# Seven-product multiplication at a second level inside the first matrix stage of an attention and feed-forward kernel

## The chip, the cores and the metric

The kernel runs on one core of a Trainium2 chip, as one program. The metric is the device time of one execution in microseconds (us), lower is better. TensorE (PE) does the matrix products, VectorE (DVE) and ScalarE (ACT) do elementwise work and read the accumulators, GpSimd (POOL) and SyncE (SP) start transfers.

## The reference

```python
kv  = einsum('bhsd,bhse->bhde', k, v)            # q, k, v: (8, 8, 576, 64)
o   = einsum('bhsd,bhde->bhse', q, kv)
x   = o / sqrt(mean(o*o, -1) + 1e-6) * g_norm    # then (B,H,S,D) -> (4608, 512)
h   = x @ w_in                                   # w_in: (512, 2048)
g   = s * max(h, 0)**2 + b
out = g @ w_out                                  # w_out: (2048, 512)
```

All is float32. Most of the arithmetic is in the two products with `w_in` (first stage) and `w_out` (second stage).

## The kernel before, in words

The 4608 tokens are cut into nine **units** of 512 tokens (`u` = 0 to 8). Each unit does the first stage, then the second. Beside it runs the attention of the next unit, as two halves A and B; each is a chain: `turn` (DVE transposes q), `product` (64 short matmuls), `back` (two DVE transposes out of PSUM), `square` (ACT), `row_sum` (DVE, then a root on ACT), `norm` (DVE), `turn_x` (DVE), `scale` (ACT).

Both stages use Strassen's scheme in Winograd's form: a 2 x 2 block product with seven products in place of eight, and sums around them. Blocks of the left matrix are combined into S1 to S4, those of the right into T1 to T4. Unit 0 multiplies plainly in the first stage. From unit 1 on the first stage has one level of the scheme: A is `w_in` transposed (A11, A12, A21, A22), B is the unit's x (B11 to B22, 256 tokens wide). The products are numbered 1 = A11 B11, 2 = A12 B21, 3 = S4 B22, 4 = A22 T4, 5 = S1 T1, 6 = S2 T2, 7 = S3 T3. The second stage of units 2 to 8 has two levels (`at_two_levels`, L878).

The first stage goes in four **steps** `s` (256 rows of each half of the result per step), each with seven **large products**. A large product (`mm1_product`) is four matmuls with a moving operand of 256 columns; the profile shows each float32 matmul as two records, so it is 8 records of 128x256. Products 1, 6, 5, 3 of a step add up in one PSUM bank x (two such banks in turn), 7 and 4 in one bank y (two in turn), 2 has its own bank z (one). Between the products on x, ACT copies the bank out (L706) and the next product on it waits for that copy. DVE makes the four blocks of the result from them (`add`, L250) and applies the squared relu (`relu_sq`, L658). The last step's products 3 and 4 are laid into the second stage (`rest`, L1137), between its first small products. There the order is: product 1 of top-level group 1 (`do_1(1)`), the large products 3 and 4, then `do_1(2)`, `do_1(6)`, `go_1(7)`, `do_1(5)`. `sums_1` makes the four sums for that group on DVE; in the kernel before it is called between the last step's products 7 and 5.

The order of the work is written out by hand: every engine takes its instructions in the order in which the program text issues them, and semaphores make it wait for another engine's instruction. `sides` (L1405) is the table that says before which product of which step each part of the attention chain is issued. The weights of the second stage come through a ring of 14 places in SBUF (`pump`, `used`), filled by transfers on SP's queue in a fixed order, a place being reused when all before it are done. Eight of the places hold k and v for `kv_product` in the units that have it (1 to 6).

Of the kernel before, what the change touches and what calls it, by code (L numbers as in the profile page):

```python
# [16 lines left out]
def kernel(  # L17
# [231 lines left out]
    def add(o, a, b):  # L249
        nc.vector.tensor_tensor(out=o, in0=a, in1=b, op=ALU.add)  # L250
# [42 lines left out]

    w2_dram = [dram.tile([P, 2, FC // 2, P], FP32, name=f"w2_{i}") for i in range(8)]
    w3_dram = [dram.tile([P, 4, FC // 4, P], FP32, name=f"w3_{i}") for i in range(8)]
    w_up = convp.tile([P, FC // 2, DM], FP32, name="w_up")
    w_dn = convp.tile([P, FC // 2, DM], FP32, name="w_dn")
    W2_AT = {
# [474 lines left out]

    ring = {}
    NR = 14

# [14 lines left out]
    for u in range(1, U):  # L793
        if u in kv_due:
            queue_w2 += [(u, "kv", (n, m)) for n in range(NP) for m in range(2)]
        if u == 1:
            queue_w2 += [(u, i, n) for i in (1, 2, 6, 7, 5, 3, 4) for n in range(2)]
        else:
            queue_w2 += [(u, i, m) for i, m in ORDER]
    next_at = [0]  # L800

# [3 lines left out]
    def pump():  # L805

        while queue_w2 and sum(map(size_of, held)) + size_of(queue_w2[0]) <= NR:
            u, i, n = key = queue_w2.pop(0)
            held.append(key)
            t = late["ring"][:, next_at[0] : next_at[0] + size_of(key)]  # L810
            next_at[0] = (next_at[0] + size_of(key)) % NR
            if i == "kv":
                load_kv_into(t[:, 0], kv_due[u], *n)
                continue
            t = t[:, :, : 2 * HN].rearrange("p q (f n) -> p q f n", n=P)
            if u == 1:
                nc.sync.dma_start(out=t, in_=w2_dram[i][:, :, 4 * n : 4 * n + 4])
                ring[key] = t
                continue
            if n <= 3:  # L820
                f = 4 if n > 1 else 0
                src = w2_dram[i][:, n // 3, f : f + 4]
            else:
                src = w3_dram[i][:, n - 4]
            nc.sync.dma_start(out=t[:, 0], in_=src)
            ring[key] = t[:, 0]
# [525 lines left out]
    def side_of(A, B, sums, u):  # L1352

        if u == 0:
            return {
                6: [lambda: kv_product(1)],
                7: [partial(A["turn"], 0), partial(A["turn"], 1)],
                8: [A["product"], A["back"], A["square"]],
                9: [A["row_sum"], partial(B["turn"], 0), partial(B["turn"], 1)],
                10: [A["norm"], A["turn_x"], A["scale"], B["product"], B["back"], B["square"]],  # L1360
                11: [B["row_sum"], B["norm"]],
                12: [B["turn_x"], B["scale"], lambda: [fn() for fn in sums_w_in(0)]],
                13: [sums],
            }
        return {
            0: [A["scale"]],
            1: [B["turn"]],
            4: [B["product"], B["back"], B["square"]],
            5: [B["row_sum"]],
            6: [B["norm"]],  # L1370
            8: [B["turn_x"], B["scale"]],
            11: [sums],
            13: [partial(loads, 3, 1)],
        }

    def loads(u, i):

        if u < U:
            for load in load_q(4 * u + 2 * i):
                load()  # L1380
# [24 lines left out]
    def sides(u, A, B):  # L1405

        first, second = {}, {}
        kv = []  # L1410
        if u in kv_due:
            kv.append(lambda: kv_product(kv_due[u]))
            kv.append(lambda: used(*((u, "kv", (n, m)) for n in range(NP) for m in range(2))))
        q = {half: [partial(loads, u + 2, half)] for half in range(2)}
        if u == 1:
            for s in range(1, NS):
                first[((0, 1), (0, 3), (1, 1))[s - 1]] = list(sums_w_in(s))
            first.update({
                (1, 3): kv,
                (2, 0): [partial(A["turn"], 0), partial(A["turn"], 1)],  # L1420
                (2, 1): [A["product"]],
                (2, 2): [A["back"]],
                (2, 3): [A["square"]],
                (3, 0): [A["row_sum"]],
                (3, 2): [A["norm"], A["turn_x"]],
                (3, 3): [lambda: [load() for load in load_q(12, rest_on=nc.sync)]],
            })
            return first, second
        if u + 1 == U:
            return first, second  # L1430
        if u == 2:
            first = {
                (0, 2): [A["turn"]],
                (0, 3): kv,
                (1, 1): [A["product"]],
                (1, 2): [A["back"], B["turn"]],
                (1, 3): [A["square"]],
                (2, 0): [A["row_sum"]],
                (2, 1): [B["product"]],
                (2, 2): [A["norm"], A["turn_x"]],  # L1440
                (2, 3): q[0],
                (3, 0): [B["back"], A["scale"]],
                (3, 1): [B["square"]],
            }
            second = {
                0: [B["row_sum"]], 2: [B["norm"]], 3: [B["turn_x"], *q[1]],
                "sums": [B["scale"]],
            }
        else:
            first = {  # L1450
                (0, 0): [A["turn"]],
                (0, 1): [A["product"]],
                (0, 2): [A["back"]],
                (0, 3): [A["square"], B["turn"]],
                (1, 0): [A["row_sum"]],
                (1, 1): kv,
                (1, 2): [A["norm"], A["turn_x"]],
                (1, 3): [B["product"], *q[0]],
                (2, 0): [B["back"], A["scale"]],
                (2, 1): [B["square"]],  # L1460
                (2, 2): [B["row_sum"]],
                (2, 3): [B["norm"]],
                (3, 0): [B["turn_x"], *q[1]],
                (3, 1): [B["scale"]],
            }
        second[5], second[6] = [[lambda n=n: x_sums(u + 1)[n]()] for n in range(2)]
        return first, second

    for u in range(U):
        A, B = pairs_of(u + 1) if u + 1 < U else (None, None)  # L1470
        if u == 0:
            first_unit()
            second = mm2(0)
        else:
            if u == 1:
                loads(2, 0)
                loads(2, 1)
            steps = [mm1(u, s) for s in range(NS)]
            first, at_second = sides(u, A, B)
            second = mm2(u, steps[-1], at_second) if u > 1 else mm2(u)  # L1480
        for s in range(NS if u > 0 else 0):
            a = steps[s]

            def at(n):
                for fn in first.get((s, n), []):
                    fn()

            at(0)
            a["x1"]()
            if s:  # L1490
                x3(steps[s - 1])
            a["z2"]()
            at(1)
            if s:
                y4(steps[s - 1])
            a["x6"]()
            at(2)
            a["y7"]()
            if s == NS - 1 and u > 1:
                second["sums"]()  # L1500
            at(3)
            a["x5"]()
        if u > 1:
            second["rest"]()
            continue
        side = side_of(A, B, lambda: [fn() for fn in x_sums(u + 1)], u)
        for n, slot in enumerate(second):
            slot()
            if u == 0:
                if n == 1:  # L1510
                    for i in range(2):
                        load_kv(1, i, convp, tag="raw", bufs=3)
                    store_w2(1)
                    loads(1, 0)
                    loads(1, 1)
                    store_w2(5)
                elif n == 2:
                    t2 = convp.tile([P, 4 * R * D], FP32, name="w_t2", tag="raw", bufs=3)
                    W2_AT[6] = t2[:, : FC // 2 * HN].rearrange("p (f n) -> p f n", n=HN)
                    for i in range(14, 16):  # L1520
                        more(i)
                    sub_w_out(6, 3, 5)
                    store_w2(3, 2, 6)
            if n == 0 and u > 0:
                x3(steps[-1])
                y4(steps[-1])
            for step in side.get(n, []):
                step()
        if u == 0:
            tc_late()  # L1530
            pump()
# [30 lines left out]
```

## Time and profile before

| what | value |
|---|---|
| median of 3 timed runs | 920.17 us (920.1 to 920.28) |
| the profiled execution | 919.9 us, its span 918.1 us |
| granted TensorE clock | 1.00 |
| PE busy | 907.6 us (99%) in 7272 matmul records |
| DVE busy | 678.2 us (74%) |
| ACT busy | 210.3 us (23%) |
| first product of units 6 and 7 | starts at 629.48 and 726.96 us: one unit is 97.48 us |
| first stage of unit 6, to the end of the last step's product 5 (629.60 to 679.50 us) | PE busy throughout; DVE 35.78, ACT 15.27 us |
| the rest of unit 6 (679.50 to 727.00 us) | PE busy throughout; DVE 37.91, ACT 4.34 us |

A row of the timeline gives start, length, engine, line, operation, tile written<-tiles read, shapes, the count of instructions merged into it and, in brackets, the idle time before it and what ended that. The length of a matmul row includes its run through the array, so the pace of PE is read from one start to the next. In the groups, the second number behind the bar is the mean time of one instruction in ns.

### The profile page before, as it was taken

The numbers are of one execution on the slowest core, as the hardware profiler recorded it, in microseconds if no ns is written. First come the engines' busy times: TensorE is split into PE (matmuls) and PEld (weight loads), VectorE is DVE, ScalarE is ACT, GpSimd is POOL, SyncE is SP. The second block draws the span as 40 slices with busy tenths as digits, with TensorE's granted clock in tenths as the row PEclk, the third lists the DMA queues.
The fourth block names the chain that finished last, engine by engine and source line by source line (L and its number), as shares of the span: only waits on it lengthen the run. The fifth ranks groups of instructions, "written<-read, shape, count | busy, mean of one in ns | idle before, by whom it ended". The sixth has DMA issues, their size and how long they took to land.

```text
span 918.1 us, 18306 instructions
## 1 busy us (share of the span) xinstructions
PE 907.6 (99%) x7272; PEld 824.6 (90%) x7272; DVE 678.2 (74%) x1149; ACT 210.3 (23%) x386; POOL 220.2 (24%) x412
## 2 busy tenths in 40 slices
PE   7999999999999999999999999999999999999998
PEld 7888888888889998899889988998899988998898
DVE  2789777687577985887677867787678768864685
ACT  3774132211124013310232023301330034002200
POOL 2000017012703242711273025603440300020000
PEclk9999999999999999999999999999999999999999
DMA  9777937249922993189416953496428800890086
GB/s 258 228 280 259 270 94 238 85 102 349 322 66 64 277 319 110 30 251 310 153 39 184 297 164 108 119 292 229 116 58 286 282 6 12 272 308 18 12 253 184
DMA packets 113605, 167.70 MB, mean 183 GB/s; under 512 B 28400, under 2 KB 45552, under 8 KB 113520
## 3 DMA queue, kind: packets, MB, share of 16 engines
q1 hardware_dynamic: 95504, 141.98, 49.4%
q0 software_dynamic: 14560, 22.31, 8.4%
q10 hardware_dynamic: 3456, 2.23, 0.9%
q8 instruction: 58, 0.95, 0.4%
q14 instruction: 27, 0.22, 0.1%
HBM read 142.35 MB, written 24.12 MB: 181 GB/s over the span
## 4 chain that ended last, share of the span: by engine, by line
PE 96%; DVE 2%; DMA 1%; ACT 0%; issue 0%; SPq 0%; DVEq 0%
PE x_ps L91 51%; PE y_ps L91 29%; PE z_ps L91 11%; PE kv_ps L380 2%; PE y_ps L559 2%; DMA kv_sb<-in_v_dram 1%; PE qT_ps L548 0%; DVE xn L469 0%; SPq L107 0%; DVE ss L459 0%; DVE o L861 0%; DVE sub L253 0%; DVE wb L245 0%; DVE xn L592 0%; DVE a L253 0%
## 5 line engine op out<-in xcount | busy, mean ns | idle before, releaser
L1380 POOL DMA_DIRECT2D q_sb<-in_q_dram x256 | 143.6, 569 | 149.6 <-issue 118.9
L706 ACT COPY r<-x_ps 128x512 f32<-128x512 f32 x96 | 56.0, 584 | 453.2 <-PE x_ps L91 423.4
L970 POOL DMA_DIRECT2D out_dram<-o x110 | 54.8, 505 | 400.7 <-DVE o L861 276.2
L91 PE MATMUL x_ps<-w_sb,sub 128*128 128x128 f32 x1176 | 149.3, 276 | 0.7 <-DVE r L861 0.7
L91 PEld LDWEIGHTS x_ps<-w_sb,sub 128*128 128x128 f32 x1176 | 139.7, 192 | 1.5 <-DVE r L861 0.9
L91 PE MATMUL x_ps<-xs,ws 128*128 128x256 f32 x512 | 122.3, 382 | 0.0
L91 PE MATMUL y_ps<-xs,wb 128*128 128x256 f32 x512 | 121.7, 380 | 0.0
L91 PEld LDWEIGHTS x_ps<-xs,ws 128*128 128x128 f32 x512 | 96.2, 190 | 16.5 <-issue 3.7
L91 PEld LDWEIGHTS y_ps<-xs,wb 128*128 128x128 f32 x512 | 96.7, 190 | 13.8 <-DVE s L250 0.4
L250 DVE TENSOR_TENSOR a<-y_ps,r 128x512 f32<-128x512 f32 x64 | 44.1, 689 | 83.2 <-ACT r L706 73.4
L91 PE MATMUL x_ps<-xT,wa 128*128 128x256 f32 x384 | 89.6, 380 | 0.1
L91 PEld LDWEIGHTS x_ps<-xT,wa 128*128 128x128 f32 x384 | 72.3, 190 | 10.1 <-ACT xT L503 0.5
L91 PE MATMUL x_ps<-w_sb,a 128*128 128x128 f32 (+1 forms) x432 | 64.9, 298 | 0.0
L91 PE MATMUL y_ps<-w_sb,a 128*128 128x128 f32 (+1 forms) x416 | 62.1, 295 | 0.0
L91 PEld LDWEIGHTS x_ps<-w_sb,a 128*128 128x128 f32 x432 | 59.0, 191 | 3.2 <-issue 0.4
L91 PE MATMUL x_ps<-xT,ws 128*128 128x256 f32 x256 | 61.2, 382 | 0.0
L91 PE MATMUL z_ps<-xT,wa 128*128 128x256 f32 x256 | 60.5, 379 | 0.0
L658 DVE SCALAR_TENSOR_TENSOR a<-a 128x512 f32<-128x512 f32 x82 | 56.7, 692 | 2.8
L91 PEld LDWEIGHTS y_ps<-w_sb,a 128*128 128x128 f32 x416 | 56.1, 192 | 2.1
L91 PEld LDWEIGHTS z_ps<-xT,wa 128*128 128x128 f32 x256 | 48.6, 190 | 6.6
L91 PEld LDWEIGHTS x_ps<-xT,ws 128*128 128x128 f32 x256 | 48.1, 190 | 6.5
L861 DVE SCALAR_TENSOR_TENSOR r<-x_ps,s_col,o 128x256 f32<-128x256 f32 (+1 forms) x84 | 34.7, 413 | 25.7 <-PE x_ps L91 24.5
(158 smaller groups left out, 1263.8 us busy)
## 6 DMA issues: line engine op xcount, KB each, us to landing
w_sb<-w SPq DMA_DIRECT2D x343, 256.0 KB, 4.8
w_raw<-in_moe_w_in_dram SPq DMA_DIRECT2D x8, 1024.0 KB, 7.3
w_raw<-in_moe_w_out_dram SPq DMA_DIRECT2D x8, 1024.0 KB, 5.2
w_sb<-w SPq DMA_DIRECT2D x14, 512.0 KB, 8.6
w<-sub POOLq DMA_DIRECT2D x28, 256.0 KB, 6.4
w_sb<-in_k_dram SPq DMA_DIRECT2D x24, 288.0 KB, 5.9
w_sb<-in_v_dram SPq DMA_DIRECT2D x24, 288.0 KB, 5.8
out_dram<-o POOLq DMA_DIRECT2D x92, 64.0 KB, 3.8
```

Of the source, the lines that this page charges most:

```text
L91: nc.tensor.matmul(o, lhsT=lhsT, rhs=rhs, start=start, stop=stop, skip_group_check=True)
L250: nc.vector.tensor_tensor(out=o, in0=a, in1=b, op=ALU.add)
L380: nc.tensor.matmul(ps[r][(r ^ l) * HB : (r ^ l) * HB + HB, i, :], lhsT=kv[l][0][rows, j, :], rhs=kv[l][1][rows, j, :], start=(j == 0), sto ...
L559: nc.tensor.matmul(ps[l][32 * p : 32 * p + 32, r, lo:hi], lhsT=bd_kv[b % 2][rows, p, at : at + 32], rhs=st["qT"][rows, p, lo:hi], start=Tr ...
L658: nc.vector.scalar_tensor_tensor(t, t, 0.0, t, ALU.max, ALU.mult)
L706: nc.scalar.copy(st[name], src)
L861: nc.vector.scalar_tensor_tensor(o, ps, s_col, other, ALU.mult, ALU.add)
L970: queues[s % 2].dma_start(out=view[b, jj, :, cols], in_=st[name, j][s * w : s * w + w, cols])
L1380: load()
```

## The change

From unit 2 on the first stage is done by a new function `mm1_deep`. Three of its large products per unit, each taken over a pair of steps, are multiplied at two levels: product 2 for the pair of steps 0 and 1 (key `(2, 0)`), product 3 for that pair (`(3, 0)`), and product 2 for steps 2 and 3 (`(2, 1)`). Each is seven **small products** of two matmuls with 128 columns (4 records). Their left sums are made once, beside unit 1's second stage, and written to DRAM (`sums_of_w_in`); six ring places per unit bring them back. Their right sums are made per unit (`sums_of_x`). All small products 1, 6, 5, 3 add up in one bank `sx`, 2, 4 and 7 in the one bank z; DVE reads these out and adds them onto what is already in the result's tile. What x1 and x5 leave in bank x is copied by ACT straight into the result's tiles. Where a block is complete only after the small products, the squared relu is two ACT instructions per step (`done_of`). The order of a pair of steps is written out in `run`, with numbered slots for the attention parts, and `sides` has new tables; `sums()` (start of `sums_1`) stands behind the last `x5`. Unit 8 has no attention work.

```diff
+    DEEP = ((2, 0), (3, 0), (2, 1))
+    def sums_of_w_in(key):
...
+        add(s1, a21, a22)
+        sub(s2, s1, a11)
+        sub(s3, a11, a21)
+        sub(s4, a12, s2)
+        for n in range(2):
+            nc.gpsimd.dma_start(
+                out=w1_dram[key][:, n], in_=t[n].rearrange("p f n -> p (f n)")
+            )
+    def mm1_deep(u):
...
+        def sums_of_x():
...
+            sub(t1, b12, b11)
+            sub(t2, b22, t1)
+            sub(t3, b22, b12)
+            sub(t4, b21, t2)
+        def x1(s):
+            st["x", s] = bank_of("x", "x")
+            mm1_product(1, u, s, st["x", s], True)
+            nc.scalar.copy(g_tile("a11", s), st["x", s])
...
+        def x5(s):
+            mm1_product(5, u, s, st["x", s], False)
+            nc.scalar.copy(g_tile("a21", s), st["x", s])
+            t = g_tile("a22", s)
+            add(t, st["y", s], ga["a21", s])
+            if s == NS - 1:
+                relu_sq_on_act(t)
+            else:
+                relu_sq(t)
...
+        def y4(s):
+            mm1_product(4, u, s, st["y", s], False)
+            t = g_tile("a12", s)
+            add(t, st["y", s], st["r2", s])
...
+        def small(i, pair, *ms):
...
+            for m in ms:
...
+                ps = st["sx" if m in (1, 6, 5, 3) else "sy"]
+                w, x = w_of(m), a[m][:, i - 2]
+                for b in range(2):
+                    matmul(ps[:, b], w[:, b], x, first and b == 0, True)
...
+                if m == 1:
+                    keep("q1", 0, 0)
+                elif m == 2:
+                    add(to(0, 0), ps, st["q1"])
+                elif m == 6:
+                    keep("q2", 1, 0)
+                elif m == 5:
+                    keep("q4", 1, 1)
+                    add(to(1, 1), st["sy"], st["q4"])
+                elif m == 3:
+                    add(to(0, 1), ps, to(0, 1))
+                elif m == 4:
+                    add(to(1, 0), ps, st["q2"])
+        def done_of(i, pair):
+            for s in (2 * pair, 2 * pair + 1):
+                relu_sq_on_act(ga[{2: "a11", 3: "a21"}[i], s])
+        def run(at, sums):
...
+            at(4)
+            y7(0)
+            small(2, 0, 6, 7)
+            at(5)
+            x5(0)
+            small(2, 0, 5)
+            at(6)
+            x6(1)
+            small(2, 0, 3, 4)
+            done_of(2, 0)
+            at(7)
+            y4(0)
+            at(8)
+            y7(1)
+            at(9)
+            x5(1)
+            at(10)
+            x1(2)
...
+            small(3, 0, 3, 4)
+            x6(3)
+            done_of(3, 0)
+            at(15)
+            small(2, 1, 1, 2)
+            x5(2)
+            at(16)
+            small(2, 1, 6, 7)
+            y7(3)
+            s1(0)
+            s1(1)
+            at(17)
+            small(2, 1, 5)
+            x3(2)
+            s3(0)
+            s3(1)
+            at(18)
+            small(2, 1, 3, 4)
+            done_of(2, 1)
+            y4(2)
+            s1(2)
+            s3(2)
+            x5(3)
+            sums()
...
+            queue_w2 += [(u, key, m) for key in DEEP for m in (6, 5)]
...
+            **{n: [partial(sums_of_w_in, key)] for n, key in zip((3, 7, 9), DEEP)},
...
             first = {
-                (0, 0): [A["turn"]],
-                (0, 1): [A["product"]],
-                (0, 2): [A["back"]],
-                (0, 3): [A["square"], B["turn"]],
-                (1, 0): [A["row_sum"]],
-                (1, 1): kv,
-                (1, 2): [A["norm"], A["turn_x"]],
-                (1, 3): [B["product"], *q[0]],
...
+                2: [A["turn"]],
+                4: [A["product"]],
+                5: [A["back"]],
+                6: [A["square"]],
+                7: [A["row_sum"], *kv],
+                8: [A["norm"], A["turn_x"]],
+                9: [B["turn"]],
+                10: [B["product"], *q[0]],
+                11: [B["back"], A["scale"]],
+                13: [B["square"]],
+                14: [B["row_sum"]],
+                15: [B["norm"]],
+                16: [B["turn_x"], *q[1]],
+                18: [B["scale"]],
             }
```

The last table is that of units 3 to 7. Unit 2 has its own, in which `turn` of B stands in slot 9 and its product in slot 12, `back` of B in slot 16.

More of the change, by code (lines that the diff above doesn't have):

```diff
@@ L295 @@
     w3_dram = [dram.tile([P, 4, FC // 4, P], FP32, name=f"w3_{i}") for i in range(8)]
+    DEEP = ((2, 0), (3, 0), (2, 1))
+    w1_dram = {key: dram.tile([P, 2, 4 * P], FP32, name=f"w1_{key[0]}{key[1]}") for key in DEEP}
     w_up = convp.tile([P, FC // 2, DM], FP32, name="w_up")
@@ L771, in mm1 @@
         )
+    def sums_of_w_in(key):
+        i, pair = key
+        w = [
+            (ws[s][:, 2] if i == 3 else wa[s][:, KH:])
+            for s in (2 * pair, 2 * pair + 1)
+        ]
+        a11, a12, a21, a22 = w[0][:, 0], w[0][:, 1], w[1][:, 0], w[1][:, 1]
+        t = [
+            late["sub"].tile([P, FC // 4, P], FP32, name="sub", tag="sub") for _ in range(2)
+        ]
+        (s2, s3), (s1, s4) = ((x[:, :2], x[:, 2:]) for x in t)
+        add(s1, a21, a22)
[6 more added lines that the diff above has]
+            )
@@ new lines, in mm1_deep, with relu_sq_on_act, x6, y7 @@
+    def mm1_deep(u):
+        st = {}
+        a = {}
+        def relu_sq_on_act(t):
+            nc.scalar.activation(t, t, AF.Relu)
+            nc.scalar.square(t, t)
+        def sums_of_x():
+            k0, k1 = (
+                xT[u][:, KH + k].rearrange("p (g q c) -> p q g c", g=2, q=2) for k in range(2)
+            )
+            b11, b12, b21, b22 = k0[:, 0], k0[:, 1], k1[:, 0], k1[:, 1]
+            t = [
+                late["sub"].tile([P, FC // 4, P], FP32, name="sub", tag="sub") for _ in range(2)
+            ]
+            (t1, t2), (t3, t4) = ((x[:, :2], x[:, 2:]) for x in t)
+            sub(t1, b12, b11)
+            sub(t2, b22, t1)
+            sub(t3, b22, b12)
+            sub(t4, b21, t2)
+            a.update({1: b11, 2: b21, 3: b22, 4: t4, 5: t1, 6: t2, 7: t3})
+        def x1(s):
+            st["x", s] = bank_of("x", "x")
+            mm1_product(1, u, s, st["x", s], True)
+            nc.scalar.copy(g_tile("a11", s), st["x", s])
+        def x6(s):
+            mm1_product(6, u, s, st["x", s], False)
+            st["r2", s] = rp.tile([P, 2, TB], FP32, name="r2", tag="ra" if s % 2 else "rb")
+            nc.scalar.copy(st["r2", s], st["x", s])
+        def y7(s):
+            st["y", s] = bank_of("y", "y")
+            mm1_product(7, u, s, st["y", s], True)
+        def x5(s):
[7 more added lines that the diff above has]
+                relu_sq(t)
+        def x3(s):
+            mm1_product(3, u, s, st["x", s], False)
+            nc.scalar.activation(ga["a21", s], st["x", s], AF.Relu)
+            nc.scalar.square(ga["a21", s], ga["a21", s])
+        def y4(s):
+            mm1_product(4, u, s, st["y", s], False)
+            t = g_tile("a12", s)
+            add(t, st["y", s], st["r2", s])
+            if s == NS - 1:
+                relu_sq_on_act(t)
+            else:
+                relu_sq(t)
+        def s1(s):
+            g_tile("s1", s)
+            g_s1(s)
+        def s3(s):
+            sub(ga["a21", s], ga["a11", s], ga["a21", s])
+        def small(i, pair, *ms):
+            name = {2: "a11", 3: "a21"}[i]
+            def to(j, h):
+                return g_pair[name, pair][:, j, :, h * P : h * P + P]
+            def w_of(m):
+                s0, s1 = 2 * pair, 2 * pair + 1
+                raw = {1: (s0, 0), 2: (s0, 1), 4: (s1, 1)}
+                if m in raw:
+                    s, k = raw[m]
+                    return ws[s][:, 2, k] if i == 3 else wa[s][:, KH + k]
+                n, k = {6: (6, 0), 7: (6, 1), 5: (5, 0), 3: (5, 1)}[m]
+                return ring[u, (i, pair), n][:, k]
+            def keep(name, j, h):
+                st[name] = late["tmp"].tile(
+                    [P, 2, P], FP32, name="r", tag="r2_2" if name == "q2" else "r14"
+                )
+                add(st[name], st["sx"], to(j, h))
+            for m in ms:
+                first = m in (1, 2, 7)
+                if m == 1:
+                    ps = ps_a.tile([P, DM], FP32, name="sx_ps", tag="x")
+                    st["sx"] = ps.rearrange("p (b c) -> p b c", c=P)[:, :2]
+                elif first:
+                    ps = bank_of(("s", m), "z", 1).rearrange("p b (m c) -> p (b m) c", c=P)
+                    st["sy"] = ps[:, :2]
+                ps = st["sx" if m in (1, 6, 5, 3) else "sy"]
+                w, x = w_of(m), a[m][:, i - 2]
+                for b in range(2):
+                    matmul(ps[:, b], w[:, b], x, first and b == 0, True)
+                if m == 7:
+                    used((u, (i, pair), 6))
+                elif m == 3:
+                    used((u, (i, pair), 5))
+                if m == 1:
+                    keep("q1", 0, 0)
[6 more added lines that the diff above has]
+                    add(to(1, 1), st["sy"], st["q4"])
+                elif m == 3:
+                    add(to(0, 1), ps, to(0, 1))
[5 more added lines that the diff above has]
+        def run(at, sums):
+            at(1)
+            x1(0)
+            at(2)
+            x1(1)
+            sums_of_x()
+            at(3)
+            small(2, 0, 1, 2)
+            x6(0)
+            at(4)
[16 more added lines that the diff above has]
+            x1(2)
+            small(3, 0, 1, 2)
+            at(11)
+            x1(3)
+            y4(1)
+            at(12)
+            small(3, 0, 6, 7)
+            y7(2)
+            at(13)
+            small(3, 0, 5)
+            x6(2)
+            at(14)
+            small(3, 0, 3, 4)
[22 more added lines that the diff above has]
+            sums()
+        last = dict(
+            x3=lambda: x3(3), y4=lambda: y4(3), x3_s1=lambda: s1(3), x3_s3=lambda: s3(3),
+            x3_square=lambda: None, y4_square=lambda: None,
+        )
+        return run, last
@@ L815, in pump @@
             t = t[:, :, : 2 * HN].rearrange("p q (f n) -> p q f n", n=P)
+            if i in DEEP:
+                nc.sync.dma_start(
+                    out=t[:, 0].rearrange("p f n -> p (f n)"), in_=w1_dram[i][:, 6 - n]
+                )
+                ring[key] = t[:, 0].rearrange("p (m b) n -> p m b n", m=2)
+                continue
             if u == 1:
@@ L1432, in sides @@
             first = {
[L1433 to L1443, printed above, removed]
+                4: [A["turn"]],
+                5: kv,
+                8: [A["product"]],
+                9: [A["back"], B["turn"]],
+                10: [A["square"]],
+                11: [A["row_sum"]],
+                12: [B["product"]],
+                13: [A["norm"]],
+                14: [A["turn_x"]],
+                15: q[0],
+                16: [B["back"], A["scale"]],
+                18: [B["square"]],
             }
@@ L1450, in sides @@
             first = {
-                (0, 0): [A["turn"]],
-                (0, 1): [A["product"]],
-                (0, 2): [A["back"]],
-                (0, 3): [A["square"], B["turn"]],
-                (1, 0): [A["row_sum"]],
-                (1, 1): kv,
-                (1, 2): [A["norm"], A["turn_x"]],
-                (1, 3): [B["product"], *q[0]],
[L1459 to L1464, printed above, removed]
+                2: [A["turn"]],
[12 more added lines that the diff above has]
+                18: [B["scale"]],
             }
@@ L1477 @@
                 loads(2, 1)
+            first, at_second = sides(u, A, B)
+            if u > 1:
+                run, last = mm1_deep(u)
+                second = mm2(u, last, at_second)
+                run(lambda n: [fn() for fn in first.get(n, [])], second["sums"])
+                second["rest"]()
+                continue
             steps = [mm1(u, s) for s in range(NS)]
-            first, at_second = sides(u, A, B)
-            second = mm2(u, steps[-1], at_second) if u > 1 else mm2(u)
+            second = mm2(u)
         for s in range(NS if u > 0 else 0):
@@ L1498 @@
             a["y7"]()
-            if s == NS - 1 and u > 1:
-                second["sums"]()
             at(3)
             a["x5"]()
-        if u > 1:
-            second["rest"]()
-            continue
         side = side_of(A, B, lambda: [fn() for fn in x_sums(u + 1)], u)
```

## The prediction

> **What bounds the kernel now.** I read the page's busy row and chain first.
>
> ```profile
> PE 907.6 (99%) x7272; PEld 824.6 (90%) x7272; DVE 678.2 (74%) x1149; ACT 210.3 (23%) x386; POOL 220.2 (24%) x412
> PE 96%; DVE 2%; DMA 1%; ACT 0%; issue 0%; SPq 0%; DVEq 0%
> ```
>
> TensorE is busy all the time and is the chain. So taking matmul time away pays in full, and any wait put into its queue costs in full. Next the PE timeline at the end of unit 6's first stage, for the pace of both kinds of product.
>
> ```profile
> 677.73 1.89 PE L91 MATMUL x_ps<-xs,ws 128*128 128x256 f32 x8
> 679.46 1.05 PE L91 MATMUL x_ps<-w_sb,a 128*128 128x128 f32 x8
> 680.35 1.99 PE L91 MATMUL x_ps<-xT,ws 128*128 128x256 f32 x8
> 682.18 1.89 PE L91 MATMUL y_ps<-xs,wb 128*128 128x256 f32 x8
> 684.80 1.06 PE L91 MATMUL x_ps<-w_sb,sub 128*128 128x128 f32 x8
> 685.70 1.06 PE L91 MATMUL y_ps<-w_sb,sub 128*128 128x128 f32 x8
> ```
>
> From one start to the next, 8 records of 256 columns take 1.73 us and 8 of 128 columns 0.893 (0.1116 each). The product at 680.35 takes 1.83: it had to wait, and a restart costs 0.10. The same view of ACT, DVE and PE shows what PE waits for:
>
> ```profile
> 679.72 0.59 ACT L706 COPY r<-x_ps 128x512 f32<-128x512 f32 x1 [2.31 <-PE x_ps L91]
> 315.13 0.34 DVE L861 SCALAR_TENSOR_TENSOR r<-x_ps,s_col,o 128x128 f32<-128x128 f32 x1
> 315.53 1.16 PE L91 MATMUL x_ps<-w_sb,sub 128*128 128x128 f32 x8 [0.66 <-DVE r L861]
> ```
>
> ACT starts its copy 0.26 us after product 5's last matmul gave way to the next, ends at 680.31, and PE goes on at 680.35. In unit 2 PE stands 0.66 us until DVE has read the bank, and the 8 records then take 0.99 to the next start at 316.52, again a restart of 0.10. So in this kernel a late reader of PSUM stops PE at once; it has been late in one place only. DVE keeps strictly to its order:
>
> ```profile
> 666.16 1.23 DVE L592 TENSOR_TENSOR xn<-q_sb,inv 128x1024 f32<-128x1024 f32 x1
> 668.25 0.69 DVE L250 TENSOR_TENSOR a<-y_ps,r 128x512 f32<-128x512 f32 x1 [0.86 <-ACT r L706]
> 668.97 0.69 DVE L658 SCALAR_TENSOR_TENSOR a<-a 128x512 f32<-128x512 f32 x1
> 669.58 1.24 DVE L603 STREAM_TRANSPOSE xT<-xn 128x1024 f32<-128x1024 f32 x1
> ```
>
> The transpose's input is ready at 667.39, yet it waits behind an addition that waits for ACT. Prices, from the groups by form:
>
> ```profile
> L658 DVE SCALAR_TENSOR_TENSOR a<-a 128x512 f32<-128x512 f32 x82 | 56.7, 692 | 2.8
> L250 DVE TENSOR_TENSOR o<-o 128x256 f32<-128x256 f32 x28 | 11.9, 425 | 1.0
> L538 DVE STREAM_TRANSPOSE qT<-q_sb 128x1024 f32<-128x1024 f32 x13 | 15.8, 1218 | 0.0
> L745 ACT ACTIVATE a<-a 128x512 f32<-128x512 f32 x7 | 4.4, 633 | 0.2
> ```
>
> Back to back, starts lie closer: 0.66 for a 512-column DVE operation (two in 1.33), 0.42 for 256, 1.21 for 1024, 1.23 for the two of `back`, 0.25 for the reciprocal, 0.66 for ACT's relu or square.
>
> **The gain.** Each unit from 2 to 8 loses 6 large products (three, over two steps each): 6 x 1.727 = 10.36. It gets 21 small ones of 4 records: 21 x 4 x 0.1116 = 9.37. That is 0.99 per unit, 6.9 in seven units. [...]
>
> **The waits.** Small products 1, 6, 5, 3 share one bank, and DVE reads each out before the next may start; before, ACT did that, and it was 23% busy. I laid DVE's and ACT's new order, as the program text issues it, beside PE's, place by place; E is the end of the large product named.
>
> (a) *Small product 3 of (2, 0).* After x5(0) ends at E, ACT copies until E+0.85, DVE adds and squares (2 x 0.66), then reads small product 5 (0.42): E+2.6. PE needs small 5 and x6(1) to get there: 0.45+1.73 = 2.17. Wait 0.5, restart 0.1: 0.6, in seven units 4.2.
>
> (b) *`product` of B, units 3 to 7.* `turn` of B now stands behind `norm` and `turn_x` of A, and these behind y4(0)'s addition. From y4(0)'s end DVE needs 0.25 + 2 x 0.66 + 0.25 + 1.21 + 1.24 + 1.21 = 5.5. PE has y7(1) and x5(1), 3.45. Wait 2.1 in five units: 10.4. Before, this `turn` had a whole step of cover (for unit 6: ended by 636.97, product at 652.26). In unit 2 three large products and two small ones lie between, and it is free.
>
> (c) *Small product 5 of (2, 1).* `done_of(3, 0)` puts four ACT instructions (4 x 0.66) behind x6(3)'s copy, ahead of that of x5(2). So x5(2), ending at E, is copied by E+1.33 and not E+0.85. DVE then adds, squares, does `turn_x` of B (1.21; in unit 2 `back`, 1.23) and only then reads small 6: E+1.35+1.33+1.21+0.42 = E+4.3. PE has two small ones and y7(3): 2.62. Wait 1.7, restart 0.1: 1.8 in units 2 to 7, 0.6 in unit 8, which has no attention: 11.4.
>
> (d) *The last step's product 3.* It waits for ACT's copy of x5(3); before, that copy just fits (680.31 against 680.35). Now it stands behind `done_of(2, 1)`, four instructions that start only after `scale` (1.7) and x3(2)'s relu and square. Counted from the end Q of wait (c): relu and square Q+2.4 to 3.7, `scale` to 5.4, `done_of` to 8.0, copy to 8.6. PE is there at Q+7.5. Wait 1.2 in units 3 to 7, 0.6 in unit 2 (`square` in place of `scale`), 0.2 in unit 8: 6.8.
>
> (e) *`do_1(5)`.* `sums` went behind x5(3), and its first instruction behind x5(3)'s addition, which waits for the same copy. DVE from Q+8.6: addition 0.66, four sums 2.65, r1 0.3, two of s2 and two of `sums_25` 2.5, addition for y4 0.7, z and r2 0.65: Q+16.1. PE, with wait (d) counted, arrives at Q+14.8. Wait 1.3, restart 0.1: 1.4 in seven units, 9.8. Before, the four sums lay at 676.37 to 678.98, and DVE had 1.35 us idle behind them.
>
> Sum of the waits: 4.2+10.4+11.4+6.8+9.8 = 42.6.
>
> **What I cost at nothing.** `sums_of_w_in`: 12 DVE operations of 0.42 and 6 POOL transfers beside unit 1's second stage, where DVE's row shows idle stretches of 4.5, 1.3 and 0.4 us between the products' reads and each bank is used again four slots of 3.45 us later; if that cover were gone, at most its 5 us. `sums_of_x`: 1.7, between the first product and small 6, where DVE is free from about 1.6 us and small 6 comes at 9.1. Six more loads of 256 KB per unit on SP: their ring places stand behind those for k and v, so they are issued some five small-product groups (4.5 us) before the unit ends and land 4.8 later (the page's median for such loads), over 8 us ahead of use; the second stage's own loads, queued behind them, start when `kv_product` is done, over 30 us ahead of use. If they were late, a transfer's 4.8 per unit, 34 in all. Small product 5 of (3, 0) clears its wait with 0.6 to spare, and L706's copies that went away were beside PE.
>
> Sum: 919.9 - 6.9 + 42.6 = 955.6 for the profiled execution; the median before lies 0.3 above that one, so **956 us**.
>
> **Rivals.**
> - *Only the count of matmuls matters* (faster): DVE is 74% busy, and its work grows by some 3 us per unit of 97 (25 new operations of 0.42, 11 fewer of 0.66). It decides if DVE and ACT reach each read 2.1 us earlier than I count, the largest of the waits; then PE never stands and 919.9 - 6.9 = 913 is left. For: one wait in the whole trace so far. Against: the queue orders above.
> - *Only the waits in front of attention parts and (a) come true*, (d) and (e) being absorbed because ACT's squares run while PE stands: 919.9 - 6.9 + 4.2 + 10.4 + 11.4 = 939.
> - *More than I count*: each change from small to large costs the restart's 0.10 even without a wait (12 stretches of small products in seven units, 8.4): 964. Against: at the unit's turn, 726.07 to 728.69, a small group is followed by a large one with 0.89 and 1.73.
> - *The gain is not there*: small products in short stretches run no faster than the large ones they replace: 956 + 6.9 = 963.
>
> **The numbers.** Forecast 0.5; 939 case 0.22; the two dearer ones 0.14 together; faster case 0.12; close to no change 0.02. The low end takes in the 939 case with its waits a fifth shorter (26.0 x 0.8: 934), rounded down to 930; the high end takes the dearer ones with the waits (c) to (e) a quarter longer (28.0 x 0.25 = 7; 964 + 7): 971. What a measurement can tell from no change is 0.2%, 1.8 us. Faster 0.12, same 0.02, slower 0.86.
>
> **What would show it.** In the new profile: PE idle in units 3 to 7 at five places, ahead of y_ps<-qT (2.1, released by DVE qT), ahead of two of sx_ps (0.5 and 1.7, DVE r), ahead of x_ps<-xT,ws (1.2, ACT a) and x_ps<-w_sb,sub (1.3, DVE r); units 3 to 7 take 97.5 - 1.0 + 7.1 = 103.6; PE busy time about 7 us less. Wrong would be: no row of PE with idle time over 0.3, or a release by DMA w_sb.

## The result, and the profile after

The changed kernel takes **951.53 us** (median of 4, 950.63 to 953.57) against 920.22 (median of 4): a ratio of 1.0342, with a 95% interval of 1.0324 to 1.036. The forecast was 956 us, range 930 to 971. The profiled execution took 951.3 us, span 949.5, granted clock 0.998; it is 31.4 us above the profiled execution of before (919.9).

The page of the changed kernel, its busy row and its chain:

```profile
PE 910.6 (96%) x7524; PEld 829.0 (87%) x7524; DVE 694.2 (73%) x1259; ACT 253.7 (27%) x463; POOL 223.8 (24%) x418
PE 78%; DVE 12%; ACT 6%; issue 2%; DMA 1%; ACTq 0%; DVEq 0%
```

The chain was 96% TensorE; now 18% of it runs over VectorE and ScalarE. Nobody is busier than TensorE, yet TensorE waits. What for, in the view of waits by engine (total, times, longest, in us):

```profile
PE y_ps L561 <- DVE qT L540: 9.9, 5, 2.0
PE sx_ps L91 <- DVE r L250: 9.3, 13, 1.3
PE x_ps L91 <- DVE r L1084: 5.8, 8, 1.0
PE x_ps L91 <- ACT a L839: 2.7, 5, 0.5
PE kv_ps L382 <- issue: 1.8, 2, 0.9
```

The first four rows are the five predicted places: (b); (a) and (c) together; (e); (d). None of them stood in before, except one of the eight waits of (e)'s row (0.7 us, unit 2). In unit 6 the timeline of PE shows them one by one:

```profile
662.68 0.71 PE L91 MATMUL sx_ps<-xT,w_sb 128*128 128x128 f32 x4 [0.29 <-DVE r L250]
...
669.61 1.89 PE L91 MATMUL x_ps<-xs,ws 128*128 128x256 f32 x8
673.48 1.36 PE L561 MATMUL y_ps<-qT,bd_kv 64*32 64x192 f32 x64 [1.98 <-DVE qT L540]
...
691.87 1.89 PE L91 MATMUL y_ps<-xs,wb 128*128 128x256 f32 x8
694.96 0.71 PE L91 MATMUL sx_ps<-sub,w_sb 128*128 128x128 f32 x4 [1.20 <-DVE r L250]
...
710.22 1.16 PE L91 MATMUL x_ps<-w_sb,sub 128*128 128x128 f32 x8 [0.64 <-DVE r L1084]
```

These are the rows of (a), (b), (c) and (e); (d) stands at 703.18, with 0.54 in its bracket. The bracket counts idle time from the modelled end of the matmul before, its run through the array included, and so is too small as a price. From start to start the large product at 669.61 gave way after 3.87 us where its pace is 1.73: (b) costs 2.14, not 1.98. Below, **gap** is the time from the last record's start to the next record's start; a gap less the usual 0.22 (after 256 columns) or 0.11 (after 128) is the wait.

### The profile page after: what moved, and what is told of

It is laid out like the page before. It is cut to its first block, busy times and chain, and to the rows that moved or that the text cites. A ratio compares the mean times of both kernels' runs of the same rounds, so it can differ in the third digit from the quotient of the medians.

```text
span 949.5 us, 19118 instructions
## 1 busy us (share of the span) xinstructions
PE 910.6 (96%) x7524; PEld 829.0 (87%) x7524; DVE 694.2 (73%) x1259; ACT 253.7 (27%) x463; POOL 223.8 (24%) x418
## 4 chain that ended last, share of the span: by engine, by line
PE 78%; DVE 12%; ACT 6%; issue 2%; DMA 1%; ACTq 0%; DVEq 0%
PE x_ps L91 40%; PE y_ps L91 23%; PE z_ps L91 7%; PE sx_ps L91 3%; DVE a L250 2%; DVE sub L253 2%; PE y_ps L561 2%; PE kv_ps L382 2%; ACT a L806 2%; DVE a L660 2%; ACT a L805 1%; ACT a L839 1%; DMA kv_sb<-in_v_dram 1%; DVE a L253 1%; ACT xT L512 1%
## 5 line engine op out<-in xcount | busy, mean ns | idle before, releaser
L91 PEld LDWEIGHTS y_ps<-xs,wb 128*128 128x128 f32 x512 | 94.5, 190 | 14.2 <-issue 2.5
L91 PEld LDWEIGHTS x_ps<-xs,ws 128*128 128x128 f32 x512 | 93.9, 190 | 11.4 <-issue 0.4
L826 ACT COPY a<-x_ps 128x512 f32<-128x512 f32 x28 | 16.4, 586 | 271.4 <-PE x_ps L91 229.7
L250 DVE TENSOR_TENSOR r<-sx_ps,a 128x256 f32<-128x256 f32 x63 | 26.3, 418 | 60.4 <-PE sx_ps L91 60.2
L250 DVE TENSOR_TENSOR a<-y_ps,r 128x512 f32<-128x512 f32 x36 | 24.8, 689 | 45.4 <-PE y_ps L91 37.7
L91 PE MATMUL y_ps<-w_sb,sub 128*128 128x128 f32 x392 | 49.5, 275 | 0.0
L253 DVE TENSOR_TENSOR a<-a,a 128x512 f32<-128x512 f32 x72 | 46.8, 684 | 0.9
L91 PE MATMUL z_ps<-w_sb,a 128*128 128x128 f32 (+1 forms) x352 | 46.8, 280 | 0.0
L91 PEld LDWEIGHTS y_ps<-w_sb,sub 128*128 128x128 f32 x392 | 46.6, 192 | 0.0
```

The lines of the kernel that those rows point to most:

```text
L91: nc.tensor.matmul(o, lhsT=lhsT, rhs=rhs, start=start, stop=stop, skip_group_check=True)
L253: nc.vector.tensor_tensor(out=o, in0=a, in1=b, op=ALU.subtract)
L826: nc.scalar.copy(g_tile("a11", s), st["x", s])
```

## The experiments

All edits are against the changed kernel; all but the last two ran beside one another on one chip, those two together on another. TensorE, VectorE and ScalarE run the same number of instructions in all of them, in another order.

**1. `turn` of B earlier.** In the table of units 3 to 7:

```diff
-                5: [A["back"]],
+                5: [A["back"], B["turn"]],
...
-                9: [B["turn"]],
```

> One entry of the table of units 3 to 7 moved: turn of B from slot 9 to slot 5, behind back of A; all else as in the changed kernel (951.5 us). Theory of the order (each wait of TensorE comes from one place in VectorE's or ScalarE's order): the five waits of 2.0 us ahead of product of B are gone, and the turn lies in an idle stretch of VectorE of 1.1 us, so nothing comes in their place: 951.5 - 5 x 2.1 = 941, and if the one stretch at half clock (3.4 us of the profile, worth 1.7) was set off by such a wait, 939.5 with a clock of 1.000. Rival, VectorE's load (the work has to be done somewhere, and a wait taken away shows up at the next read): 950 to 952, with the waits ahead of small products 3 and 5 longer by together 2 us per unit. Rival, the small products themselves are dear: no change.

Measured 938.96 us, 1.0203 of before (1.0188 to 1.0218). The row `y_ps L561 <- DVE qT L540` is gone, and the others stand as they were:

```profile
PE sx_ps L91 <- DVE r L250: 9.3, 13, 1.3
PE x_ps L91 <- DVE r L1084: 5.8, 8, 1.0
PE x_ps L91 <- ACT a L839: 2.7, 5, 0.5
```

The profiled executions differ by 951.3 - 938.78 = 12.5. Five waits of 2.14 are 10.7; the granted clock went from 0.998 to 1.000, which is 1.7 more (see the hardware section). So (b) is one misplaced VectorE instruction per unit, and taking it forward cost nothing elsewhere: the rival that VectorE's load would come due at another place is refuted for this wait.

**2. `scale` of B out of the way of `done_of`.**

```diff
-                18: [B["scale"]],
             }
+            second[0] = [B["scale"]]
```

> One entry of the table of units 3 to 7 moved: scale of B from slot 18 to the second stage (slot 0 there). Theory of the order: ScalarE's 1.6 us of scale stand ahead of the squares of done_of(2, 1) and so ahead of the copy that the last step's product 3 waits for; without them the copy is ready when TensorE arrives. The wait of 0.6 us ahead of that product goes in five units, the later one ahead of do_1(5) shrinks by some 0.1: 951.5 - 3.5 = 948. Rival, VectorE's load: the additions behind the copy are what is late, so do_1(5) waits 0.6 longer and the time stays 951 to 952.

Measured 949.49 us, 1.0324 (1.0304 to 1.0344). (d) is gone, yet only 2.0 us came off. That is within the spread of the two kernels' runs, so the size rests on the profiled executions (951.3 to 949.61) and on the gaps in them. The same row of waits that stood at 5.8 in the changed kernel now reads, in this one, and unit 6's timeline of PE shows its part in it:

```profile
PE x_ps L91 <- DVE r L1084: 7.7, 8, 1.0
```

```profile
710.60 1.16 PE L91 MATMUL x_ps<-w_sb,sub 128*128 128x128 f32 x8 [1.01 <-DVE r L1084]
```

(e)'s bracket of 0.64 has become 1.01 (its gap 0.91 has become 1.29). What was late at (d) was ScalarE's copy; what is late at (e) is VectorE's queue of additions and sums behind it. With (d) gone TensorE arrives 0.7 earlier, and VectorE only partly. About half of the wait removed came back at the next read: the gain that the theory gave did not come in full, and the rival held for that half.

**3. VectorE's load around (e) moved later.** In `rest`, with more calls of `s2` and the sums behind it shifted by as much:

```diff
             step["x3_square"]()
-            s2((0, 1))
-            sums_25((7,))
             step["y4"]()
...
             step["x3_s1"]()
+            sums_25(())
+            s2((0,))
             go_1(7)
             do_1(5)
+            s2((1,))
             sums_25((5, 6), 2)
```

> Only the order in the second stage's start is changed: two of s2's subtractions and the two sums for go_25(7), 2.65 us of VectorE, stand behind do_1(5) in place of ahead of the read of do_1(6). Theory of the order: VectorE reads do_1(6) that much earlier, and the wait of 0.8 us with its restart ahead of do_1(5) goes in seven units: 951.5 - 6.5 = 945. Rival, VectorE's load: the 2.65 us come due a few products later, where VectorE is 80% busy, and waits of some 1 us appear ahead of do_25(6) or go_25(7): 951.

Measured 950.52 us, 1.0329 (1.0309 to 1.0348): nearly nothing gained. (e) is gone ahead of `do_1(5)`, but the same kind of wait stands 20 us later, ahead of `do_6(5)`, in seven units (in unit 2 the kernel before already had a shorter one there). PE and DVE of this kernel in unit 6:

```profile
729.30 1.16 PE L91 MATMUL x_ps<-w_sb,sub 128*128 128x128 f32 x8 [0.57 <-DVE r L1084]
```

```profile
726.93 0.68 DVE L250 TENSOR_TENSOR sub<-a,a 128x512 f32<-128x512 f32 x1
727.64 0.69 DVE L253 TENSOR_TENSOR sub<-sub,a 128x512 f32<-128x512 f32 x1
728.25 0.48 DVE L1084 SCALAR_TENSOR_TENSOR o<-y_ps,s_col,r 128x256 f32<-128x256 f32 x1
728.64 0.34 DVE L1084 SCALAR_TENSOR_TENSOR o<-z_ps,s_col,r 128x128 f32<-128x128 f32 x1
728.90 0.34 DVE L1084 SCALAR_TENSOR_TENSOR r<-x_ps,s_col,o 128x128 f32<-128x128 f32 x1
```

The read that TensorE waits for ends at 729.24; VectorE runs without a pause before it, and two sums of 512 columns stand in that queue. The load was put off, not given room: the rival was right again, though the waits came at a later read than the two it named. The sum over the profiled executions agrees: -7.0 for (e), +6.4 for the new waits (0.74 in six units, 1.3 in unit 2, restarts), +1.7 for a second stretch at half clock, -1.1 for a gap in `kv_product` that did not come, together 0; measured 951.1 - 951.3 = -0.2.

**4. All five at once.** Experiment 3's `rest`; `turn` of B as in 1; the rest of B's chain (product to scale) one to four slots earlier, unit 2 likewise; `turn_x` of A one slot later; and the squared relu of steps 0 and 2 and the first two `s1` set where VectorE has time, with `s3` and the third `s1` moved a little as well (`x5(s, False)` leaves its squared relu to the line behind). Some of the lines:

```diff
             at(5)
-            x5(0)
+            x5(0, False)
             small(2, 0, 5)
+            relu_sq(ga["a22", 0])
...
             small(2, 1, 1, 2)
-            x5(2)
-            at(16)
+            s1(0)
+            s1(1)
+            x5(2, False)
             small(2, 1, 6, 7)
+            relu_sq(ga["a22", 2])
             y7(3)
-            s1(0)
-            s1(1)
...
```

> All orders changed together: turn of B early as before this run; the rest of B's chain moved from slots 10 to 18 to between slots 9 and 14, ahead of where the small products crowd; the square of the first and third block a22 put behind the read of small product 5 or 6; s1 of steps 0 and 1 ahead of x5(2); the second stage's start as in the run before this. Instructions are the same but for their order. Theory of the order: all five waits are gone, and what is left is the gain in matmuls: 919.9 - 6.9 = 913, up to 917 with a wait or two left over, clock 1.000: faster than the kernel before. Rival, VectorE's load: some 2 us of wait per unit stay, 925 to 935. Rival, the small products in short stretches cost more than their pace in long ones: 920 or more although no wait is seen.

Measured 921.83 us (median of 10), 1.0017 (1.0007 to 1.0026). All five waits are gone; 30 us came back, not 35 to 38. What is left is experiment 3's new one, in the view of waits:

```profile
PE x_ps L91 <- DVE r L1083: 5.4, 7, 2.0
```

Its gaps are 0.85 in units 3 to 8 (0.74 of wait each, 4.4 in all) and 2.27 in unit 2, where the kernel before already had 0.94. So the expectation missed by one VectorE read that the re-ordering itself had made late.

**5. The two squared relus alone.** The changed kernel with only these lines of experiment 4:

```diff
-            x5(0)
+            x5(0, False)
             small(2, 0, 5)
+            relu_sq(ga["a22", 0])
...
-            x5(2)
+            x5(2, False)
...
             small(2, 1, 6, 7)
+            relu_sq(ga["a22", 2])
```

> The changed kernel with two VectorE instructions per unit moved: the squared relu of block a22 of step 0 behind the read of small product 5 of (2, 0), and that of step 2 behind the read of small product 6 of (2, 1); 0.66 us each. Theory of the order: the wait ahead of small product 3 (0.45 and a restart of 0.1, seven units, 3.9) goes, and that ahead of small product 5 of (2, 1) falls from 1.36 to 0.7 (six units, 4.0; gone in the last unit, 0.3): 951.5 - 8.2 = 943. Rival, VectorE's load: the squares come due behind it, and the waits ahead of product of B, of the last step's product 3 or of do_1(5) grow: 947 to 951.

Measured 946.21 us, 1.0279 (1.0265 to 1.0293). (a) is gone and (c) went from a gap of 1.58 to 0.85, one squared relu's length less; the row of waits shows both, and (e) and (d) did not grow:

```profile
PE sx_ps L91 <- DVE r L250: 2.9, 6, 0.5
PE x_ps L91 <- ACT a L839: 2.7, 5, 0.5
```

That is 3.9 for (a) and 4.4 for (c) (0.73 in six units): 943.0 was due for the profiled execution and 945.97 came. It held three stretches at half clock against one, 2 x 1.7 = 3.4 more; of the 0.4 that this is too much, 0.3 is (c) in unit 8, which is gone as well.

**6. The wait of experiment 4 taken away.** Experiment 4, with the two sums of `sums_73` that stood ahead of that read set behind it, and unit 2's last attention parts of B one slot later (the lines shown are against experiment 4):

```diff
             do_25(3)
-            sums_73((5, 6), 7)
             do_25(4)
...
             do_6(5)
+            sums_73((5, 6), 7)
             sums_73((5, 6), 3)
```

> The run with all orders changed (921.8 us), in which the one wait left is VectorE's read of do_6(6) ahead of do_6(5) (0.74 us in six units, 2.2 in unit 2, restarts with them): the two sums for go_73(7), which nothing needs until 8 us later, are put behind do_6(5), and in unit 2 norm and turn_x of B go one slot later. Theory of the order: 921.8 - 6 x 0.84 - 1.4 to 2.2 = 915, faster than the kernel before, and what separates it from 913 are the gap inside one or two of the kv products and one wait ahead of y7. Rival, VectorE's load: another read is late by 0.5 us or more in each unit, 918 to 922.

Measured **914.53 us** (median of 5), 0.9935 of before (0.9922 to 0.9949): faster than both. Its busy row, and its one wait on a PSUM read:

```profile
PE 902.4 (99%) x7524; PEld 827.9 (91%) x7524; DVE 695.9 (76%) x1259; ACT 254.5 (28%) x463; POOL 223.5 (24%) x418
```

```profile
PE x_ps L91 <- DVE r L1083: 0.7, 1, 0.7
```

That wait is as long as the one of the kernel before, and in the same unit 2, but it is not the same one: there it stood at 315.53, ahead of `do_6(5)`; here `do_6(5)` starts without a wait, and it stands at 333.45, ahead of the unit's fourth last product, where the kernel before shows none. Here too a wait was put off to a later read.

With the same number of matmuls and of DVE and ACT instructions as in the changed kernel, 37 us are gone. The count of matmuls gives 919.9 - 6.9 = 913.0; the profiled execution took 915.06, and two gaps (0.68 inside unit 3's `kv_product`, 0.55 between two large products on y in unit 4) are 1.2 of the 2.1 between. Of the other 0.9, 0.4 had come before unit 2's first stage (it starts at 239.24 here, at 238.83 before), and some 0.5 comes from two shorter delays in unit 2's second stage (at 303.47 and 324.30). Units 5, 6 and 7, which have no gap in either kernel, show the gain by itself: they take 96.34, 96.44 and 93.81 us where the kernel before takes 97.38, 97.48 and 94.84, so 1.03 to 1.04 less each, where the prediction counted 0.99. The order alone could not have given that, since the kernel before has no wait in these units to lose. So the gain of the change is real, 5.7 us between the medians, and was covered by the order.

## Why the prediction was right

The sign, the mechanism and the five places came as predicted; the sum came out 4 us too high. Part of that closeness is luck: (c), (d) and (e) together were 7.7 too high, and 3.7 that the prediction did not have (the last two rows above the sum) made up half of it. By its steps, over the seven units, in the changed kernel's profile:

| step | predicted | measured |
|---|---|---|
| gain of fewer matmul columns | -6.9 | -6.9 taken; experiment 6 shows 1.03 to 1.04 in each of units 5 to 7, and 5.7 in all |
| (a) small product 3 of (2, 0) | 4.2 | 3.9: gaps of 0.67, so a wait of 0.45, and a restart of 0.1, in seven units |
| (b) `product` of B | 10.4 | 10.7: gaps of 2.35 or 2.36 in five units |
| (c) small product 5 of (2, 1) | 11.4 | 9.2: gaps of 1.58 in five units (1.65 in unit 2, 0.45 in unit 8), and restarts |
| (d) the last step's product 3 | 6.8 | 4.1: gaps of 0.82 in five units and restarts, none in units 2 and 8 |
| (e) `do_1(5)` | 9.8 | 7.0: gaps of 0.91 in five units, 1.18 in unit 2, 1.29 in unit 8, and restarts |
| half clock | none | 1.7 |
| gaps inside `kv_product`, units 3 and 5 | none | 2.0 |
| sum | 35.7 | 31.7 (951.3 - 919.9 = 31.4) |

**(b)** came within 0.3 us. The prediction's own terms for it add up to 5.48 and so to a wait of 2.03, not 2.1; measured it is 2.14, and the 0.15 in which TensorE goes on after VectorE's last instruction, which the sum left out, is most of the difference. The queue of DVE in unit 6 shows the working:

```profile
668.09 0.69 DVE L250 TENSOR_TENSOR a<-y_ps,r 128x512 f32<-128x512 f32 x1 [2.65 <-PE y_ps L91]
668.81 0.69 DVE L660 SCALAR_TENSOR_TENSOR a<-a 128x512 f32<-128x512 f32 x1
669.42 0.25 DVE L592 RECIPROCAL inv<-rms 128x16 f32<-128x16 f32 x1
669.70 1.23 DVE L594 TENSOR_TENSOR xn<-q_sb,inv 128x1024 f32<-128x1024 f32 x1
670.96 1.25 DVE L605 STREAM_TRANSPOSE xT<-xn 128x1024 f32<-128x1024 f32 x1
672.13 1.20 DVE L540 STREAM_TRANSPOSE qT<-q_sb 128x1024 f32<-128x1024 f32 x1
```

VectorE stood idle for 2.65 us until y4(0) released its addition, then six instructions went without a pause, and TensorE goes on at 673.48, 0.15 after the last one's end. That transpose could have run before that idle stretch: it only stood behind an instruction that waited.

**(c), (d), (e)** were over-sized, mostly by one term: I took ScalarE's relu and square at 0.66 apart. In the changed kernel ScalarE shows:

```profile
689.04 0.63 ACT L805 ACTIVATE a<-a 128x512 f32<-128x512 f32 x1
689.71 0.63 ACT L806 ACTIVATE a<-a 128x512 f32<-128x512 f32 x1
690.25 0.61 ACT L805 ACTIVATE a<-a 128x512 f32<-128x512 f32 x1
690.89 0.63 ACT L806 ACTIVATE a<-a 128x512 f32<-128x512 f32 x1
691.43 0.57 ACT L839 COPY a<-x_ps 128x512 f32<-128x512 f32 x1
```

This reading was wrong: only the square, which reads what the relu wrote, comes 0.64 to 0.67 behind it; what follows a square and does not read it starts after 0.54. The trace of before already had 0.47 or 0.48 from the start of a ScalarE copy to that of an instruction right behind it. The four take 2.39 and not 2.64, and the copy ends at 692.00, 1.02 after x5(2)'s end and not 1.33. In (d) the same chain is shorter again: the copy ends at 703.13, 8.2 after wait (c) and not 8.6. In (e) VectorE is done with the read at 710.17 (15.2 after wait (c), not 16.1): 0.4 from that copy, and the rest because its sums, too, start 0.60 to 0.72 apart where I took 0.66 for each. TensorE, with the smaller (d), comes 0.4 earlier, so 0.8 is left where I had 1.3.

**Rivals.** "Only the count matters" gave 913 and named its condition, that DVE and ACT reach the reads 2.1 us earlier. In this order they do not; in experiment 6 they do, and the time is 914.5. The 939 case fell, since (d) and (e) did come, smaller. The dearer case of a restart at each change of size fell: small products and a large one without a wait follow, from 657.44 in unit 6, after 0.44, 0.45 and 1.73. That the gain is not there fell with experiment 6. More and shorter matmul records, each with a weight load of its own, did not cost time here: 7524 records and 7524 loads in experiment 6 in place of 7272 and 7272 in the kernel before, and 5.7 us less.

**What the prediction had wrong**: "PE busy time about 7 us less". It rose by 3.0, because the modelled end of the matmul ahead of each wait counts, and because of the slow clock; in experiment 6, with one wait left, it fell by 5.2. Units 3 to 7 were to take 103.6; from one (a) to the next, units 3 to 6 take 103.3, 102.35, 103.3 and 102.3, the longer two being those that hold a gap in `kv_product` of 1.1. For unit 7 the 97.5 it started from was wrong: that unit has no `kv_product` and takes 94.84 in the kernel before.

**Left open:** why `kv_product` has a gap in some units. It falls in a run of 144 short matmuls while SP issues nine or ten loads; the profile names now "issue", now a transfer of v. It came in units 3 and 5 in the changed kernel and in experiments 1, 2 and 5, in unit 3 alone in experiments 3, 4 and 6, and not in before. No experiment tests it.

## What to carry to other kernels

Here a change that trades matmul columns for more reads of PSUM by VectorE was priced by the order of VectorE's and ScalarE's queues, not by their busy share (73% and 27%, with 32 us of waits). So, for every read that TensorE waits for, count what stands ahead of it in its engine's program order and compare that with what TensorE has to do meanwhile. A wait that is taken away comes due at a later read if the engine behind it has no slack there (experiments 2 and 3, and unit 2 of 6), so re-order all the places of one engine together, and put work that is ready early into the stretches where that engine idles, ahead of an instruction that waits. Then look in the new profile for the read that the re-ordering itself made late (experiments 4 and 6: 7 us for two sums and a few parts of unit 2).

## What the runs showed of the hardware that was not expected

After some waits TensorE runs at half clock for a while. The changed kernel, unit 7 (start, busy of PE, PEld, DVE, ACT, POOL with counts, granted clock, DMA share, GB/s), and PE's timeline there:

```profile
768.00:773.30 5.30, 3.33 (x17) 2.62 (x17) 5.20 (x7) 1.46 (x4) 0.00 (x0) 1.00 0.02 7
773.30:778.00 4.70, 4.70 (x42) 3.48 (x43) 1.12 (x2) 0.05 (x1) 0.00 (x0) 0.64 0.00 0
778.00:782.00 4.00, 4.00 (x24) 3.61 (x24) 2.07 (x4) 3.48 (x7) 0.00 (x0) 1.00 0.01 4
```

```profile
773.29 1.10 PE L561 MATMUL y_ps<-qT,bd_kv 64*32 64x256 f32 x32 [1.97 <-DVE qT L540]
774.32 3.59 PE L91 MATMUL x_ps<-xT,wa 128*128 128x256 f32 x8
```

A large product, whose row is 1.89 long elsewhere, is 3.59 long here (3.39 from its start to the next, where the pace is 1.73), and a mean clock of 0.64 over 4.70 us is 4.70 x 0.36 / 0.5 = 3.4 us at half (the trace's record of the clock has 0.50 from 774.55 to 777.97), which costs 1.7. In the profiled executions it came one time in the changed kernel, one in experiment 2, two in 3 and three in 5 (whose waits (b) are the same): 7 times for 20 waits (b). The stretch shown here begins 1.3 us after its wait's end. In those executions it did not come after the waits of 1.4 us or less, nor after experiments 3's and 4's waits of 2.2 in unit 2, and not in before or in experiments 1 and 6, while TensorE had matmuls left. So in these four kernels a wait of 2.1 us cost 2.1 and, in 7 cases of 20, 1.7 more. The idle time before it here is 1.97 us by the trace (2.14 from start to start).

Which of the waits it follows was not shown. The waits (b) are all 1.97 or 1.98 us of idle time, with half clock behind them or without. It also changes from one execution to the next of one kernel: of the ten of experiment 4, whose longest wait is that of 2.2 in unit 2, four have a granted clock of 1.000 (920.34 to 921.6 us, the profiled one among them) and six 0.998 (921.69 to 923.2). No experiment was made to vary a wait's length or its place.
